# Expert weights converted through four staging pairs, an early list from 24 token tiles, and a second weight set asked for on its own

## The chip, the core and the metric

The kernel runs on one core of a Trainium2 chip. The metric is the device time of one execution in microseconds (us), taken as the median of several runs. A profiled execution, from which all rows come, is a run of its own and takes a little longer.

## What is computed

The reference chains three parts in float32:

```python
# 1 attention between x (8, 8, 512, 64) and 32 state rows per head, both ways
xread = softmax(scale * x @ state.T) @ state
sread = softmax(scale * state @ x.T) @ x
x = concat([xread, sread], rows)       # 8 * 544 = 4352 tokens of 512
# 2 a feed-forward layer: w_in (512, 2048), w_out (2048, 512)
g = relu(x @ w_in) ** 2
x = g @ w_out
# 3 one of 8 experts per token: w1 (8, 512, 1024), w2 (8, 1024, 512)
idx = argmax(cosine(x, expert_emb) / tau); gate = softmax(...)[idx]
out[token] = gate * (relu(x[token] @ w1[idx]) @ w2[idx])
```

The kernel keeps float32 accuracy by splitting each operand into two float16 halves, high and low, and adding three matmuls (high by high, high by low, low by high).

## The kernel before

The tokens lie in 34 tiles of 128: 32 of the x rows (NXT) and two of the state rows. Three stages overlap.

The attention goes through eight batches (`attention`, `state_side`). The first mixture (`up1`, `down1`) goes through 17 units of two token tiles: the up product of a unit in eight chunks c, the squared hidden chunk split into `g_h` and `g_l` by `hidden` (L1130 and L1136 on ScalarE, L1139 and L1141 on VectorE), and the down product of each tile in four pieces of 12 matmuls (L1219 to L1221). The last unit holds the state rows; its up product is L1174 to L1176. `route_tile` scales a finished tile into a record (`rec`), turns it with a DMA transpose into `xr` (L1017, one buffer, queue of SyncE) and forms the expert logits on TensorE (L1026 to L1028). `route_group` takes four tiles at once: some 30 small VectorE operations choose the expert and the place, advance the running counts `cum`, and GpSimd scatters the four records into device memory (L1105).

The second mixture (`moe2`) takes 128 tokens of one expert per step. `list_of` makes three lists of steps from the counts: list 0 with the first EARLY = 6 full tiles, taken from the first SEEN token tiles alone, list 1 with the other full tiles, list 2 with the rests in halves of 64. `gather` fetches the records of a step (L1456), `turn` transposes them (L1476), `up2` and `down2` multiply (L1527 to L1529, L1552), `finish` scales and scatters the result (L1504). Even steps use weight places of side 0 (`stage` for w1, `he` for w2), odd steps those of side 1 (`xx` and `sw`). `fetch_weights` loads them with SyncE: it reads the expert's number from the list and issues a 2 MB load that is skipped if the expert is the one already there (L1436).

`experts` brings w1 and w2 into the split form that `fetch_weights` reads. It loads halves of 1 MB into staging places (`stage`, one part of `wo_t`, and after the attention `xx`), finds a scale per matrix (L936), and converts 64 pieces of 128 by 1024: ScalarE makes the high half (L308), VectorE the low half (L303), both into a pair of buffers in the first half of `he` (`phl`, two pairs), and SyncE writes both halves, 256 KB each, to device memory (L325). A pair is free again when its write has landed. The second half of `he` belongs to the attention (`eb_v`) until that is over.

The order on every engine is fixed at build time by a planner (`Plan`). Each part of the kernel is a thread that yields (engine, duration); the planner always takes the thread that can start first, at a tie the one with the lower priority number. Events (`ev`) and slots order the threads, and `plan.dma(bytes)` books a transfer at 350 GB/s and 2 us to land. "attention" is the event after the last batch, "experts" that after the last conversion, "spare" that the part of `wo_t` in which the lists are computed is free, "moe1" that after the last down product. The priority number of the conversions is PRIO_E (4) during the attention and PRIO_E1 after it; routing has 2 and the lists 2.5.

Of the kernel before, what the change touches and what calls it, by code (L numbers as in the profile page):

```python
# [11 lines left out]
F16 = mybir.dt.float16  # L12
# [12 lines left out]
NT = NTOK // 128  # L25
NXT = B * S // 128
EARLY = 6
SEEN = 28
FULL = -(-(NTOK - NE * 127) // 128)
HT = 64  # L30
HALF = (NTOK - 128 * FULL + NE * (HT - 1)) // HT // 2 + 1
# [20 lines left out]
MARG = 1.75  # L52
GATE_E = ('xg', 1)
PRIO_E = 4
PRIO_E1 = 1.6
PRIO_SW = 1.4
TINY = 0.18

# [152 lines left out]
def act(n):  # L211
    return "act", 0.1 + 0.83e-3 * n
# [19 lines left out]
def moe_kernel(  # L232
# [19 lines left out]
    plan = Plan()  # L252
# [52 lines left out]
    def split(hi, lo, src, scale, n):  # L305

        yield act(n)
        nc.scalar.activation(out=hi, in_=src, func=AF.Copy, scale=scale)  # L308
        yield dve(n)
        split_lo(lo, src, scale, hi)  # L310
# [12 lines left out]
    def load(dst, src, nbytes):  # L323
        yield "sp", 0.06
        nc.sync.dma_start(dst, src)  # L325
        return plan.dma(nbytes)
# [35 lines left out]
    cum = const.tile([128, NT + 1, NE], F16, name="cum")  # L362
# [17 lines left out]
    def ev(*key):  # L380
        return evs.setdefault(key, Ev(plan))
# [7 lines left out]
    he = att.tile([128, 4096], I32, name="he")  # L389
# [4 lines left out]
    phl = he[:, 0:2048].bitcast(F16).rearrange("p (q a n) -> p q a n", q=2, a=2)  # L394
# [305 lines left out]
    stage_slots, phl_slots, pjk_slots = Slots(plan, 3), Slots(plan, 2), Slots(plan, 1)  # L700
# [167 lines left out]
    def tensor_scale(acc, s, inv):  # L868

        v = small.tile([128, 1], F32, name="fv")  # L870
        yield tiny(1)
        V.tensor_reduce(out=v, in_=acc, axis=X, op=ALU.add)
        at = plan.now()
        yield t_slots
        plan.cur[2] = max(at, plan.now())
        p = ps_t.tile([128, 512], F32, name="t")
        yield "pe", 0.1
        mm(p[:, 0:1], lhsT=one32, rhs=v, start=True, stop=True)
        w = small.tile([128, 1], F32, name="fw")
        yield tiny(4)  # L880
        V.tensor_scalar(out=w, in0=p[:, 0:1], scalar1=FLOOR, scalar2=None, op0=ALU.max)
        t_slots.release()
        pow2(s, inv, w, 204)


    def experts():


        yield ev(*GATE_E)
        halves = {}  # L890
        last = wo_t[:, NB:].rearrange("p q a k d -> p (q a k d)").bitcast(I32)
        places = [stages[0], stages[1], last]

        def put(t):
            if t is last and ev("attention").time is not None:
                ev("spare").set()
            else:
                places.append(t)
                stage_slots.release()

        def more():
            yield ev("attention")
            for i in range(2):
                put(xx[:, 2048 * i:2048 * i + 2048])

        def fetch():
            for n in range(4 * NE):
                yield stage_slots
                e, h = n // 4, n % 2
                t = places.pop(0)  # L910
                if t is last and ev("attention").time is not None:
                    put(t)
                    yield stage_slots
                    t = places.pop(0)
                halves[n] = t
                t = t.bitcast(F32)
                if n % 4 < 2:
                    v = w1[e].rearrange("(k p) f -> p k f", p=128)[:, 2 * h:2 * h + 2, :]
                else:
                    v = w2[e].rearrange("(k p) f -> p k f", p=128)[:, 4 * h:4 * h + 4, :]  # L920
                when = yield from load(t.rearrange("p (k f) -> p k f", k=v.shape[1]), v, 1 << 20)
                ev("stage", n).set(when)

        def scale():
            for i in range(2 * NE):
                acc = small.tile([128, 4], F32, name="pacc")
                if ev("attention").time is not None:
                    plan.cur[1] = PRIO_E1
                for n in range(2 * i, 2 * i + 2):
                    yield ev("stage", n)  # L930
                    for a in range(2):
                        yield pjk_slots
                        jk = att.tile([128, 1024], BF16, name="pjk")
                        col = 2 * (n % 2) + a
                        yield act(1024)
                        nc.scalar.activation(out=jk, in_=halves[n].bitcast(F32)[:, a * 1024:a * 1024 + 1024],  # L936
                                             func=AF.Square, accum_out=acc[:, col:col + 1])
                        pjk_slots.release()
                col = i // 2 + NE * (i % 2)
                yield from tensor_scale(acc, se[:, col:col + 1], ise[:, col:col + 1])  # L940
                ev("scale", i).set()

        plan.add(fetch(), PRIO_E)
        plan.add(more(), PRIO_E)
        plan.add(scale(), PRIO_E)
        for i in range(2 * NE):
            e, col = i // 2, i // 2 + NE * (i % 2)
            dst = (w1_d if i % 2 == 0 else w2_d)[e * 128:e * 128 + 128, :]
            yield ev("scale", i)
            if ev("attention").time is not None:  # L950
                plan.cur[1] = PRIO_E1
            for q in range(4):
                n = 2 * i + q // 2
                src = halves[n].bitcast(F32)[:, q % 2 * 1024:q % 2 * 1024 + 1024]
                at = plan.now()
                yield phl_slots
                plan.cur[2] = max(at, plan.now())
                hl = phl[:, q % 2]
                yield from split(hl[:, 0, :], hl[:, 1, :], src, se[:, col:col + 1], 1024)
                if q % 2 == 1:  # L960
                    put(halves.pop(n))
                at = plan.now()
                yield from load(dst[:, q * 1024:q * 1024 + 1024], hl[:, 0, :], 1 << 18)
                t = yield from load(dst[:, 4096 + q * 1024:4096 + q * 1024 + 1024], hl[:, 1, :], 1 << 18)
                phl_slots.release(t)
                plan.cur[2] = at
        ev("experts").set()

# [437 lines left out]
    def sides_of(t):  # L1406
        which, j = order[t]
        return (2, 3) if which == 2 else ((j + (EARLY if which else 0)) % 2,)

    def fetch_weights(t0, t1):  # L1410
        def fetch(name, done, ts, slots, src):
            last = None
            for t in ts:
                which, j = at_step(t)
                yield ev("tab", which)
                tab = lists[which]["tab"]
                if last is not None:
                    yield ev(done, last)
                elif which == 2:
                    last = HALF_AT - 6 if name == "w1" else HALF_AT - 5  # L1420
                    yield ev("moe1")
                    yield ev(done, last)
                else:
                    yield ev("experts")
                    yield ev("attention")
                    if name == "w2":
                        yield ev("up", 2 * B - 1)
                sides = sides_of(t)
                for i, a in enumerate(sides):
                    if i and last + 1 < t:  # L1430

                        yield ev(done, last + 1)
                    yield "sp", 0.15
                    ex = nc.sync.value_load(tab[0:1, i, j:j + 1], min_val=0, max_val=NE - 1)
                    new = nc.sync.value_load(tab[0:1, 2 + i, j:j + 1], min_val=0, max_val=1)
                    nc.sync.dma_start(slots[a], src[bass.ds(ex * 128, 128)], cond=new)  # L1436
                    when = plan.dma(2 << 20 if j == 0 and which != 1 else 1 << 19 if which == 2 else 1 << 18)
                last = t
                ev(name, t).set(when)

        for a in range(3):
            ts = [t for t in range(t0, t1) if sides_of(t)[0] == a]
            plan.add(fetch("w1", "up2", ts, w1s, w1v), 3)
            plan.add(fetch("w2", "down2", ts, w2s, w2v), 3)
# [3 lines left out]
    def gather(t0, t1, m2):  # L1448
        for t in range(t0, t1):
            which, j = at_step(t)  # L1450
            yield ev("idx", which)
            yield ev("records", (NT if which else SEEN) - 1)
            yield rec2_slots
# [6 lines left out]

            need = puts[:SEEN] if which == 0 else puts
            for put in need:
# [118 lines left out]
    def switch():  # L1581

        yield ev("cum", SEEN - 1)
        yield ev("spare")
        fetch_weights(0, NMAIN)
        yield from list_of(0, EARLY, SEEN)
        yield ev("up", 2 * B)
# [87 lines left out]
```

## Time and profile before

| | us |
|---|---|
| median of 3 runs (1145.3 to 1145.65) | 1145.32 |
| profiled execution | 1157.43 |
| its span, first to last instruction | 1155.6 |
| TensorE busy | 1032.8 (89%) |
| VectorE busy | 708.0 (61%) |
| ScalarE busy | 583.3 (50%) |

PE is TensorE's matmuls, PEld its weight loads, DVE VectorE, ACT ScalarE, POOL GpSimd, SP SyncE, SPq a queue entry of SyncE. Matmuls overlap, so the duration of one is longer than the step from one start to the next, and a busy share says less than the steps. The granted clock is a share of full speed (2.4 GHz); 0.50 is the lower level, 1.2 GHz. In brackets behind an instruction stands how long its engine was idle before it and whose end it waited for.

### The profile page before, as it was taken

Reading aid. Unit: us, or ns where it says so; the run is one execution under the profiler, and the core shown is the slowest. Engines: PE = TensorE matmul, PEld = TensorE weight load, DVE = VectorE, ACT = ScalarE, POOL = GpSimd, SP = SyncE. Lnnn points to the kernel's source line nnn. Section 1 sums busy time; section 2 is a strip of 40 time slices with the busy share of each in tenths; the row PEclk is TensorE's granted clock in tenths of the full one; section 3 lists DMA queues with packets and bytes.
Section 4 is the critical chain, followed back from the end, with each engine's and each line's share of the span. In section 5 each row is a group of like instructions: output and inputs, shape, how many; then the busy total and the mean of one; then the engine's idle time right before and its main releaser. Section 6 shows DMA issues by size and latency. Waiting matters only on the chain. (4 is left out here: it accounts for less than half of the span.)

```text
span 1155.6 us, 26458 instructions
## 1 busy us (share of the span) xinstructions
PE 1032.8 (89%) x10707; PEld 665.2 (58%) x10707; DVE 708.0 (61%) x1838; ACT 583.3 (50%) x959; POOL 126.2 (11%) x149
## 2 busy tenths in 40 slices
PE   2255899999999999999999999699999999999995
PEld 1134356555555555565555666377776777767773
DVE  6998877968869878688696784356422222222221
ACT  6689777776776977677777873111111111101110
POOL 0200000200100201002001010212121211211201
PEclk8579799999999999999999999899999999999998
DMA  9345466566685685656736676634696777685690
GB/s 354 112 151 128 151 159 211 105 193 145 183 223 125 209 238 157 189 117 183 238 71 229 205 232 273 167 92 93 209 297 173 204 213 206 185 250 155 179 295 28
DMA packets 160546, 211.77 MB, mean 183 GB/s; under 512 B 112226, under 2 KB 113506, under 8 KB 155171
## 3 DMA queue, kind: packets, MB, share of 16 engines
q1 hardware_dynamic: 152098, 182.94, 55.5%
q0 software_dynamic: 8320, 27.08, 7.2%
q8 instruction: 86, 1.41, 0.5%
q14 instruction: 42, 0.34, 0.1%
HBM read 257.92 MB, written 51.68 MB: 268 GB/s over the span
## 5 line engine op out<-in xcount | busy, mean ns | idle before, releaser
L1219 PE MATMUL d<-wo_t,g_h 128*128 128x512 f16 x544 | 209.7, 386 | 3.6 <-DVE g_h L1139 1.4
L1221 PE MATMUL d<-wo_t,g_l 128*128 128x512 f16 x544 | 209.3, 385 | 1.8 <-DVE l L1063 1.8
L1220 PE MATMUL d<-wo_t,g_h 128*128 128x512 f16 x544 | 209.5, 385 | 1.2 <-DVE wo_t L303 1.2
L1486 ACT ACTIVATE r<-u 128x512 f32<-128x512 f32 x70 | 41.8, 597 | 324.5 <-PE u L1529 300.0
L1167 PE MATMUL u<-aT,sw 128*128 128x256 f16 x512 | 141.5, 276 | 25.3 <-ACT r L1130 22.5
L1169 PE MATMUL u<-aT,sw 128*128 128x256 f16 x512 | 141.4, 276 | 0.9 <-DVE sw L303 0.9
L1168 PE MATMUL u<-aT,sw 128*128 128x256 f16 x512 | 141.3, 276 | 0.0
L1130 ACT ACTIVATE r<-u,cg 128x512 f32<-128x512 f32 x136 | 93.0, 684 | 72.9 <-PE u L1176 35.4
L1489 DVE CAST hh<-r 128x512 f16<-128x512 f32 x70 | 30.4, 434 | 136.5 <-ACT r L1486 134.4
L1105 POOL DMA_INDIRECT rec_d<-rec,pi x34 | 37.8, 1112 | 576.6 <-DVE f L1009 175.7
L1141 DVE TENSOR_TENSOR g_l<-r,g_h 128x512 f16<-128x512 f32 x136 | 93.3, 687 | 6.5 <-ACT r L1136 5.1
L1500 DVE TENSOR_SCALAR o<-d,rec,wo_t 128x512 f32<-128x512 f32 x35 | 28.3, 810 | 108.9 <-PE d L1552 99.2
L1221 PEld LDWEIGHTS <-g_l 128*128 128x128 f16 x544 | 53.9, 99 | 70.2 <-issue 5.3
L1552 PEld LDWEIGHTS <-hh 128*128 128x128 f16 (+1 forms) x688 | 54.7, 102 | 56.9 <-issue 0.4
L1136 ACT ACTIVATE r<-r 128x512 f32<-128x512 f32 x136 | 85.6, 629 | 1.9
L1219 PEld LDWEIGHTS <-g_h 128*128 128x128 f16 x544 | 54.2, 100 | 55.9 <-issue 5.7
L1220 PEld LDWEIGHTS <-g_h 128*128 128x128 f16 x544 | 53.8, 99 | 53.5 <-issue 5.0
L1139 DVE CAST g_h<-r 128x512 f16<-128x512 f32 x120 | 50.9, 424 | 47.8 <-ACT r L1136 44.7
L1527 PE MATMUL u<-xes,stage 128*128 128x128 f16 x448 | 75.9, 219 | 0.0
L1529 PE MATMUL u<-xes,stage 128*128 128x128 f16 x448 | 75.9, 219 | 0.0
L1528 PE MATMUL u<-xes,stage 128*128 128x128 f16 x448 | 75.9, 219 | 0.0
L1168 PEld LDWEIGHTS <-sw 128*128 128x128 f16 x512 | 50.6, 99 | 37.6 <-issue 26.5
(334 smaller groups left out, 2682.3 us busy)
## 6 DMA issues: line engine op xcount, KB each, us to landing
w_d<-he SPq DMA_DIRECT2D x128, 256.0 KB
wo_t<-w_d SPq DMA_DIRECT2D x16, 2048.0 KB
stage<-w_d SPq DMA_DIRECT2D x14, 2048.0 KB
he<-w_d SPq DMA_DIRECT2D x14, 2048.0 KB
xx<-w_d SPq DMA_DIRECT2D x13, 2048.0 KB
sw<-w_d SPq DMA_DIRECT2D x13, 2048.0 KB
stage<-in_w_dram SPq DMA_DIRECT2D x20, 1024.0 KB
g_h<-w_d SPq DMA_DIRECT2D x8, 2048.0 KB
```

The source lines that it names most:

```text
L1130: nc.scalar.activation(out=r, in_=ps, func=AF.Relu, scale=cg[:, g:g + 1])
L1136: nc.scalar.activation(out=r, in_=r, func=AF.Square)
L1141: V.tensor_tensor(out=gl, in0=r, in1=gh, op=ALU.subtract)
L1167: mm(o, lhsT=hl[:, i, 0, fs], rhs=aT[:, i, :], start=i == 0, stop=False)
L1168: mm(o, lhsT=hl[:, i, 0, fs], rhs=aT[:, 2 + i, :], start=False, stop=False)
L1169: mm(o, lhsT=hl[:, i, 1, fs], rhs=aT[:, i, :], start=False, stop=i == 1)
L1219: mm(ps, lhsT=g_h[:, f, ts], rhs=w[:, 0, :], start=f == 0, stop=False)
L1220: mm(ps, lhsT=g_h[:, f, ts], rhs=w[:, 1, :], start=False, stop=False)
L1221: mm(ps, lhsT=g_l[:, f, ts], rhs=w[:, 0, :], start=False, stop=f == KF - 1)
L1527: mm(p[:, j, xs], lhsT=w[:, 0, k, fs], rhs=xe[:, k, xs], start=k == 0, stop=False)
L1528: mm(p[:, j, xs], lhsT=w[:, 0, k, fs], rhs=xe[:, 4 + k, xs], start=False, stop=False)
L1529: mm(p[:, j, xs], lhsT=w[:, 1, k, fs], rhs=xe[:, k, xs], start=False, stop=k == 3)
```

## The change

`experts` views the whole of `he` as four half pairs instead of the first half as two. A deque `pairs` hands them out: 0 and 1 from the start, 2 and 3 are added with one slot each when the attention is over. PRIO_E1 goes from 1.6 to 2.2 and SEEN from 28 to 24. In `fetch_weights` the first load of w1 for step 1 waits, in the plan, for the counts of the last x tile ("cum" of NXT - 1), and that of w2 for "moe1"; before, both followed the same events as those of step 0. The planner books all four first loads of steps 0 and 1 with 2 MB, and the first loads of list 2 with 0.5 MB; before, 2 MB were booked for the first step of lists 0 and 2 and 0.25 MB for step 1.

```diff
-SEEN = 28
+SEEN = 24
-PRIO_E1 = 1.6
+PRIO_E1 = 2.2
@@ experts
+        halves_of = he.bitcast(F16).rearrange("p (q a n) -> p q a n", q=4, a=2)
+        pairs = deque((0, 1))
@@ more
             for i in range(2):
                 put(xx[:, 2048 * i:2048 * i + 2048])
+                pairs.append(2 + i)
+                phl_slots.release()
@@ the conversion of a piece
-                hl = phl[:, q % 2]
+                pair = pairs.popleft()
+                hl = halves_of[:, pair]
...
                 phl_slots.release(t)
+                pairs.append(pair)
@@ fetch_weights
                     if name == "w2":
                         yield ev("up", 2 * B - 1)
+                    if t == 1:
+
+                        yield ev("moe1") if name == "w2" else ev("cum", NXT - 1)
...
-                    when = plan.dma(2 << 20 if j == 0 and which != 1 else 1 << 19 if which == 2 else 1 << 18)
+                    when = plan.dma(2 << 20 if t < 2 else 1 << 19 if which == 2 else 1 << 18)
```

## Rows read from the trace of the kernel before

**Rows 1.** The page: span, and PE's busy tenths in 40 equal slices

```profile
span 1155.6 us, 26458 instructions
...
PE   2255899999999999999999999699999999999995
```

**Rows 2.** Table by slice: busy PE, PEld, DVE, ACT, POOL; clock; DMA share; GB/s

```profile
606.70:635.60 28.90, 26.32 (x213) 14.95 (x211) 19.13 (x42) 20.93 (x35) 3.02 (x7) 0.94 0.68 229
635.60:664.50 28.90, 28.69 (x208) 18.54 (x207) 21.42 (x60) 25.64 (x44) 0.00 (x0) 1.00 0.67 205
664.50:693.40 28.90, 28.69 (x199) 18.05 (x197) 24.72 (x89) 20.64 (x32) 4.61 (x7) 1.00 0.74 232
...
722.20:751.10 28.90, 18.79 (x116) 10.00 (x115) 10.14 (x51) 5.12 (x10) 6.28 (x7) 0.82 0.66 168
```

**Rows 3.** Timeline of PE around 725 us: start, duration, engine, line, operation

```profile
725.50 0.27 PE L1176 MATMUL u<-x_h,wi_l 128*128 128x256 f16 x1
732.63 0.19 PE L1026 MATMUL t<-en_h,xr 128*128 128x8 f16 x1 [6.85 <-DMA xr<-rec]
...
732.97 0.59 PE L1219 MATMUL d<-wo_t,g_h 128*128 128x512 f16 x1
...
736.63 0.38 PE L1219 MATMUL d<-wo_t,g_h 128*128 128x512 f16 x1
```

**Rows 4.** Timeline of SyncE's queue, 690 to 735 us

```profile
691.69 12.73 SPq L325 DMA_DIRECT2D w_d<-he  x8
706.47 0.37 SPq L1436 DMA_DIRECT2D stage<-w_d  x1
...
712.72 21.65 SPq L1017 DMA_TRANSPOSE xr<-rec  x2
```

**Rows 5.** Table by 2 us, columns as in Rows 2

```profile
720.00:722.00 2.00, 2.00 (x17) 1.51 (x16) 0.00 (x0) 0.09 (x1) 0.00 (x0) 1.00 1.02 426
...
726.00:728.00 2.00, 0.00 (x0) 0.00 (x0) 0.00 (x0) 0.00 (x0) 0.00 (x0) 1.00 0.98 384
...
734.00:736.00 2.00, 2.00 (x6) 0.70 (x5) 0.00 (x0) 0.00 (x0) 0.00 (x0) 0.50 0.68 131
```

**Rows 6.** Timelines of ACT, DVE and PE, 741 to 750 us

```profile
742.13 0.63 ACT L1136 ACTIVATE r<-r 128x512 f32<-128x512 f32 x1
...
741.69 0.17 DVE L1031 COPY lg<-t 128x8 f32<-128x8 f32 x1 [0.37 <-PE t L1028]
...
743.91 0.42 DVE L1139 CAST g_h<-r 128x512 f16<-128x512 f32 x1
...
746.09 0.68 DVE L1141 TENSOR_TENSOR g_l<-r,g_h 128x512 f16<-128x512 f32 x1
...
744.39 0.39 PE L1219 MATMUL d<-wo_t,g_h 128*128 128x512 f16 x1 [1.42 <-DVE g_h L1139]
...
746.83 0.61 PE L1221 MATMUL d<-wo_t,g_l 128*128 128x512 f16 x1 [1.84 <-DVE l L1063]
...
750.19 0.38 PE L1220 MATMUL d<-wo_t,g_h 128*128 128x512 f16 x1
```

**Rows 7.** The waits of the whole span: us in total, times, longest

```profile
PE u L1167 <- ACT r L1130: 22.5, 18, 2.8
```

**Rows 8.** Conversions after the attention: first on ACT, last on DVE

```profile
612.74 1.14 ACT L308 ACTIVATE he<-stage,se 128x1024 f16<-128x1024 f32 x1
...
702.77 1.28 DVE L303 SCALAR_TENSOR_TENSOR he<-xx,se,he 128x1024 f16<-128x1024 f32 x1
```

**Rows 9.** Timeline of PE: last down product, first uses of xx, third tile, sw

```profile
761.83 0.38 PE L1221 MATMUL d<-wo_t,g_l 128*128 128x512 f16 x1
...
765.40 0.22 PE L1527 MATMUL u<-xes,xx 128*128 128x128 f16 x1
...
776.29 0.22 PE L1527 MATMUL u<-xes,stage 128*128 128x128 f16 x1
...
781.68 0.38 PE L1552 MATMUL d<-sw,hh 128*128 128x512 f16 x1
```

## The prediction

> **What bounds the kernel now.** I began with the page. Its line of 40 slices shows TensorE (PE) at 9 nearly everywhere between the first five slices and the last; the one hole is the slice at 722 to 751 us [rows 1]. The table by slice gives its size: 18.79 us of PE work in 28.90 us at a mean granted clock of 0.82, where the slices before are full at 1.00 or nearly so [rows 2]. VectorE (DVE) and ScalarE are not full there, so this stretch is bound by PE, and a change to the weights can pay only through this hole. I went through the starts of all matmuls and counted as loss what a step from one start to the next takes beyond the usual 0.216 us (512 columns) or 0.11 us (256). From 612 to 722 us that finds four losses of 0.3 to 0.5 us, after 752 us ten of about 0.5, in the hole two large ones.
>
> Stall one runs from 725.50 to 732.63 us: PE wants the turned rows of token tile 30 (L1026) and waits for the transpose (xr<-rec) [rows 3]. On the queue of SyncE (SP) that transpose was issued at 712.72, right behind four weight loads of 2 MB, the first at 706.47 [rows 4]. The transfers run at 384 to 426 GB/s up to 728 us [rows 5]; 8.39 MB at some 410 GB/s are 20.5 us, most of the delay. PE loses 7.0 us (7.13 less 0.11), and afterwards it runs at clock 0.50, that is 1.2 of 2.4 GHz [rows 5]: nine matmuls from 732.97 to 736.63 take 3.66 us instead of 1.94 [rows 3]. Together 8.7 us.
>
> Stall two is DVE's doing. The logits of tile 31 come at 741.69, and the small routing operations of tiles 28 to 31 are put ahead of the split of the last hidden chunk (743.91 and 746.09), for which PE waits 1.42 and 1.84 us by the rows, 1.6 and 2.0 by the starts. Eight matmuls from 746.83 then take 3.36 us instead of 1.73 [rows 6]. Together 5.2 us. Without routing work 0.75 us would stay: ScalarE's square ends at 742.76, the cast (0.42) lets PE start at about 743.25 where it ran out at 742.81, and the subtract (0.68) holds it about 0.3 us more [rows 6].
>
> **The change part by part.** The plan that orders the instructions is the same until the attention is over, at about 612 us: the new half pairs and the priority act only from there on, and list 0 waits for "spare" besides. So the first 612 us cost and give nothing.
>
> *First weights of side 1 asked for apart.* Loads three and four (into xx and sw) leave their place ahead of tile 30's transpose. Ahead of it then stand 4.19 MB, 10.2 us at 410 GB/s: from 706.47 to about 717. The transpose landed some 4 us after the last load (728 to 732.6), so now near 721.5, and PE comes to L1026 at 725.61. Stall one is gone with 4 us to spare, even if nothing else moves: +8.7 us. The planner now books these two loads as 2 MB each, where it booked 0.25 MB each, 1.5 us for what takes 10.2. That is why it put L1026 too early. The loads' time on SP (four in 6.25 us [rows 4], so 1.6 each) leaves that place too.
>
> *Where they land.* w1 of step 1 now follows "cum" of tile 31, about 728 to 738 us, and takes 1.6 on SP, 5.1 of transfer and some 2 to land. PE first wanted xx at 765.40, so about 11 us earlier in the new run: 754.5. w2 follows "moe1", the last down matmul, at 761.83 before and 751 after, so it lands at 760; PE wanted sw at 781.68, now about 771 [rows 9]. Behind w2 on SP stand the transposes of tile 33 and of the third expert tile; the latter would land at about 761, and PE wants it at 776.29 less 11, 765.4 [rows 9]. I cost this at nothing; what hides it is the PE work of steps 0 and 1, with 4 us to spare at the tightest place. If that cover is gone it is rival C. The Trainium skill ("DMA: Bandwidth & Descriptors", section "Queues, rings and completion order") speaks against this part: a DMA engine consumes the descriptors of a ring in order, so a load asked for later still holds up all that is queued behind it. The trace agrees (the transpose of 712.72 waited out all four loads [rows 4]). By that rule alone the 10.2 us are moved and not removed, and the sum is rival C's; by the rows PE has other work at the new place, and the sum stands.
>
> *Four pairs instead of two, priority 2.2 instead of 1.6.* After the attention 19 pieces are converted from 612.74 to 704.05, one in 4.8 us [rows 8], and the last eight writes go out from 691.69 on [rows 4]. A piece costs 1.14 us of ScalarE and 1.28 us of DVE [rows 8] for any number of pairs; the new pairs take away the wait for a pair's write. DVE is idle for 9.8, 7.5 and 4.2 us of the slices from 606.70 on [rows 2]. Packed into half of that, the last piece is done about 10 us earlier, at 694 (bounds: 704, no gain, and 683, no idle time left). On PE this is worth nothing by itself, as the second mixture begins later. Its price is that denser conversions come in the way of the hidden chunks' work. Over the whole span PE waited for L1130 18 times, 22.5 us in all, 2.8 at most, and nearly always during the attention [rows 7]; after it, once, 0.2 us. I take -1.0 us, nearer to the stretch after the attention; bounds 0 and -4, a mean wait of 1.25 us in each of three slices. The routing of tiles 24 to 27, which gave way to the conversions at 1.6, now goes ahead of them; nobody waits for its records before the first gather at 741.65, so that is worth nothing.
>
> *Early list from 24 tiles.* "cum" of tile 23 is there before the attention ends, so the list starts with "spare", at about 623 us, and is in time for a first load at 694 or later, as it was for that at 706.47. It is the same work, and by the reference's inputs all six early tiles are of expert 0 for 24 tiles as for 28: lists and switches of weights are unchanged. The gathers wait for the pool that opens after the last up product, as before. Zero. The third list's first loads, booked as 0.5 MB instead of 2, don't reorder PE, for which the second mixture is one thread: zero, bounds +-0.5 us.
>
> *Stall two.* Tile 31's transpose waits for tile 30's L1026 (one buffer), so its logits came 9 us after 732.63. With stall one gone they come while PE is one or two chunks further back, and the small operations (21 at 0.2 us) meet a chunk behind which PE has a down product of 2.6 us in hand. Bounds: all 5.2 us stay, or 0.75. I take 2.0 us left, nearer to the floor, since the meeting came of the late transpose: +3.2 us.
>
> **Sum.** 8.7 + 3.2 - 1.0 = 10.9 us. The profiled execution took 1157.43 us (the span of 1155.6 and 1.8 around it), and would take 1146.5. The median of the runs, 1145.32, is 12.1 us lower; PE's steps are the same in both, so I take off the same microseconds: 1134.4, forecast 1134.5.
>
> **Rivals.**
> A: stall two stays whole, as the planner again lets the routing start just before the last chunk: 8.7 - 1.0 = 7.7, so 1137.6. For it: such operations run as soon as they are ready, in the order of the plan. Against: the same coincidence is needed.
> B: the conversions crowd out the hidden chunks: the longest wait seen (2.8 us [rows 7]) in each of three slices, 8.4 us, and stall two unchanged: 8.7 - 8.4, so about 1145, no change. Against: after the attention PE mostly has the other unit's down product to turn to.
> C, the slower end: the two moved loads stand ahead of transposes for which PE has already come. Each is 5.1 us of queue, both 10.2, and two spells at 1.2 GHz cost 3.3 more (1.7 and 1.6 above), against 8.7 saved: -4.8, so 1150. It decides once PE's work after the last down product runs short by more than the 4 us above.
> D: the pairs don't speed the conversions, because DVE or the transfers set their pace. Stall one still goes (the 4 us at tile 30), nothing crowds, but the routing shifts less and 4 us of stall two stay: 8.7 + 1.2 = 9.9, so 1135.5.
>
> **How the numbers follow.** Forecast 0.50, A 0.18, D 0.12, B 0.10, C 0.10. The range leaves out C and most of B: from both stalls down to the floor (8.7 + 4.45, and the small losses after 612 us, 1131) up to A with the crowding at its bound (8.7 - 4 = 4.7, 1140.6) and a part of B: 1131 to 1142. A measurement of this kernel tells 0.2% (2.3 us) from no change. Faster by more: forecast, A, D and a little of B, 0.82; within: most of B, 0.08; slower: C, 0.10.
>
> **What would show it.** Right: no wait of L1026 for xr<-rec above 1 us between 700 and 770; on SP two weight loads, then transposes, then the loads of xx and sw singly; a full clock at 722 to 751; the last conversion near 694. Wrong: first up products that wait for xx, sw or xes; waits for L1130 that add up between 612 and 700; PE at clock 0.50 in a new place.

## The result, and the profile after

The changed kernel takes 1133.99 us (median of 4 runs, 1130.1 to 1137.14) where the kernel before takes 1145.49 beside it (4 runs, 1145.3 to 1152.02): a ratio of 0.9876 with a 95% interval of 0.9841 to 0.9911. Measured again in 5 rounds beside the first experiments, the ratio is 0.9861 (0.9831 to 0.9891). The profiled execution took 1136.58 us. Behind the edits in `experts`, line numbers of the changed kernel stand 6 to 9 higher (L1026 is L1032, L1130 is L1136, L1219 to L1221 are L1225 to L1227, L1436 is L1445, L1527 is L1536).

The page of the changed kernel, and its table by slice with the columns of [rows 2]:

```profile
span 1134.7 us, 26451 instructions
...
PE   2245799999999999999999999999999999999995
...
606.70:635.60 28.90, 27.28 (x220) 15.82 (x216) 22.11 (x72) 18.94 (x30) 2.80 (x5) 1.00 0.72 216
...
722.20:751.10 28.90, 28.90 (x288) 19.97 (x286) 14.63 (x63) 7.52 (x15) 10.55 (x11) 1.00 0.84 200
```

The hole of [rows 1] is closed: PE is full from 722 to 751 us at clock 1.00, where it had 18.79 us of work at 0.82 [rows 2]. SyncE's queue shows the new order, tile 30's transpose ahead of the first loads, tile 31's between the second and the third:

```profile
696.76 1.26 SPq L1023 DMA_TRANSPOSE xr<-rec  x1
698.44 0.85 SPq L325 DMA_DIRECT2D w_d<-he  x2
701.46 0.37 SPq L1445 DMA_DIRECT2D stage<-w_d  x1
703.54 0.35 SPq L1445 DMA_DIRECT2D he<-w_d  x1
712.44 1.26 SPq L1023 DMA_TRANSPOSE xr<-rec  x1
715.75 0.35 SPq L1445 DMA_DIRECT2D xx<-w_d  x1
...
741.00 0.36 SPq L1445 DMA_DIRECT2D sw<-w_d  x1
```

On the timeline of PE, from 612 us to the early steps of the second mixture (784 us), there is one wait of more than a microsecond, for ScalarE, and one small one for a transpose. Tiles 30 and 31 (704.55 and 719.17) pass without a wait:

```profile
621.06 0.27 PE L1173 MATMUL u<-aT,sw 128*128 128x256 f16 x1 [1.62 <-ACT r L1136]
...
704.55 0.17 PE L1032 MATMUL t<-en_h,xr 128*128 128x8 f16 x1
...
719.17 0.17 PE L1032 MATMUL t<-en_h,xr 128*128 128x8 f16 x1
...
752.67 0.18 PE L1032 MATMUL t<-en_h,xr 128*128 128x8 f16 x1 [0.54 <-DMA xr<-rec]
```

Stall two is gone too. On VectorE (DVE) the logits of tile 31 come 8 us before the split of the last hidden chunk (L1145), and the routing of tiles 28 to 31 has advanced its counts (L1082) before that split:

```profile
719.79 0.16 DVE L1037 COPY lg<-t 128x8 f32<-128x8 f32 x1
...
726.42 0.76 DVE L1082 TENSOR_TENSOR cum<-cum,oh 128x8 f16<-128x8 f16 x4
...
727.69 0.42 DVE L1145 CAST g_h<-r 128x512 f16<-128x512 f32 x1
```

To compare kernels I count PE's loss as the prediction did: what a step from one matmul's start to the next takes beyond the usual one for its columns, from 26 us after the start of tile 24's squares to the ninth r of the second mixture. It was 15.8 us and is now 3.9. The two profiled executions lie 20.9 us apart (1157.43 and 1136.58), more than the medians. Some 12 us of that are this loss; 2.3 us are there before the two programs differ in order (tile 24's squares start at 588.57 and 586.32 us), and the rest lies around 605 to 612 us and in short pauses of the second mixture, which come and go between executions.

### The profile page after: what moved, and what is told of

Same layout as the page of the kernel before. It is cut to its first block, busy times and chain, and to the rows that moved or that the text cites. A ratio compares the mean times of both kernels' runs of the same rounds, so it can differ in the third digit from the quotient of the medians.

```text
span 1134.7 us, 26451 instructions
## 1 busy us (share of the span) xinstructions
PE 1025.5 (90%) x10707; PEld 663.7 (58%) x10707; DVE 706.3 (62%) x1838; ACT 583.1 (51%) x959; POOL 128.1 (11%) x149
## 5 line engine op out<-in xcount | busy, mean ns | idle before, releaser
L1225 PE MATMUL d<-wo_t,g_h 128*128 128x512 f16 x544 | 207.6, 382 | 1.7 <-ACT wo_t L862 0.8
L1226 PE MATMUL d<-wo_t,g_h 128*128 128x512 f16 x544 | 207.4, 381 | 1.2 <-DVE wo_t L303 1.2
L1227 PE MATMUL d<-wo_t,g_l 128*128 128x512 f16 x544 | 207.2, 381 | 0.0
L1136 ACT ACTIVATE r<-u,cg 128x512 f32<-128x512 f32 x136 | 92.6, 681 | 53.4 <-PE u L1175 33.5
L1227 PEld LDWEIGHTS <-g_l 128*128 128x128 f16 x544 | 53.5, 98 | 66.6 <-issue 3.1
L1225 PEld LDWEIGHTS <-g_h 128*128 128x128 f16 x544 | 53.9, 99 | 53.0 <-issue 3.2
L1145 DVE CAST g_h<-r 128x512 f16<-128x512 f32 x120 | 50.7, 423 | 41.2 <-ACT r L1142 41.0
L1536 PE MATMUL u<-xes,stage 128*128 128x128 f16 x448 | 75.9, 219 | 0.0
```

Source lines behind the costliest of these rows:

```text
L1136: nc.scalar.activation(out=r, in_=ps, func=AF.Relu, scale=cg[:, g:g + 1])
L1225: mm(ps, lhsT=g_h[:, f, ts], rhs=w[:, 0, :], start=f == 0, stop=False)
L1226: mm(ps, lhsT=g_h[:, f, ts], rhs=w[:, 1, :], start=False, stop=False)
L1227: mm(ps, lhsT=g_l[:, f, ts], rhs=w[:, 0, :], start=False, stop=f == KF - 1)
L1536: mm(p[:, j, xs], lhsT=w[:, 0, k, fs], rhs=xe[:, k, xs], start=k == 0, stop=False)
```

## The experiments

All ratios are to the kernel before on the same chip in 5 rounds. Its median there was 1159.88 us in the first group, 1155.54 in the second and 1145.76 in the third. The losses are each of one profiled execution.

### First group: the loads, and what is left without them

**The two edits of the loads alone**, on the kernel before:

```
+                    if t == 1:
+                        yield ev("moe1") if name == "w2" else ev("cum", NXT - 1)
...
-                    when = plan.dma(2 << 20 if j == 0 and which != 1 else ...
+                    when = plan.dma(2 << 20 if t < 2 else ...
```

> The kernel before with the two edits of fetch_weights alone: side 1's first loads wait in the plan, and the planner books 2 MB for each first load. Pairs, priority and early list as before. Theory Q (the two loads queued ahead of tile 30's transpose make the hole, and stall two follows from the late transpose): stall one goes, 8.7 us, and 0 to 4.5 us of stall two, so 1132 to 1137. Theory R (what counts is that the expert weights are ready sooner, so pairs, priority and list make the gain): under 1 us of gain, 1144 or more.

Measured: 0.9981 (0.9956 to 1.0005), loss 13.35 us. The ratio is theory R's, no clear gain, but not for its reason: tile 30 no longer waits, stall two stays, and tile 32 waits instead. PE, then SyncE's queue:

```profile
730.40 0.39 PE L1219 MATMUL d<-wo_t,g_h 128*128 128x512 f16 x1 [0.95 <-DVE g_h L1139]
732.86 0.61 PE L1221 MATMUL d<-wo_t,g_l 128*128 128x512 f16 x1 [1.86 <-DVE g_l L1141]
...
752.52 0.19 PE L1026 MATMUL t<-en_h,xr 128*128 128x8 f16 x1 [3.32 <-DMA xr<-rec]
```

```profile
735.73 0.33 SPq L1439 DMA_DIRECT2D xx<-w_d  x1
736.44 3.55 SPq L1479 DMA_TRANSPOSE xes<-rec  x1
741.05 4.81 SPq L1017 DMA_TRANSPOSE xr<-rec  x1
```

The load of xx went out at 735.73 us and stands ahead of tile 32's transpose: the mechanism of rival C, at a place where I had not looked for a reader. GpSimd's four scatters of records run at the same time (742.54 to 747.45 us); their share in this wait was not measured apart. The clock falls with it (by 2 us, columns as in [rows 2]):

```profile
750.00:752.00 2.00, 0.00 (x0) 0.00 (x0) 0.00 (x0) 0.00 (x0) 0.00 (x0) 1.00 0.99 208
752.00:754.00 2.00, 1.48 (x24) 1.48 (x25) 0.60 (x5) 0.00 (x0) 0.00 (x0) 0.60 1.12 293
754.00:756.00 2.00, 2.00 (x23) 2.00 (x22) 0.99 (x2) 1.17 (x2) 0.00 (x0) 0.55 0.94 401
```

**The changed kernel without these two edits** (pairs, priority and early list stay; the diff is the one above, reversed).

> The changed kernel without the two edits of fetch_weights: four pairs, priority 2.2 and the list from 24 tiles stay, the four first loads stand in one row again. Theory Q: the row is issued some 5 us earlier, as the conversions end earlier (first load at 701.5 in the changed kernel against 706.5), so stall one shrinks from 8.7 to some 2 to 5 us and stall two may stay: 1137 to 1142. Theory R: the whole gain is here, 1133 to 1136.

Measured: 0.9941 (0.9916 to 0.9967), loss 12.35 us. The four loads stand in a row from 699.73 to 705.55 and tile 31's transpose behind them, so the long wait is back, one tile later; stall two is gone. The ratio is in theory Q's range, with the parts the other way round: Q had stall one shrink and let stall two stay:

```profile
725.92 0.19 PE L1032 MATMUL t<-en_h,xr 128*128 128x8 f16 x1 [7.04 <-DMA xr<-rec]
```

**The booking alone.** The plan counts 2 MB for the loads of step 1, and nothing waits that did not wait before:

```
-                    when = plan.dma(2 << 20 if j == 0 and which != 1 else ...
+                    when = plan.dma(2 << 20 if t == 1 or j == 0 and which != 1 else ...
```

> The kernel before with the booking alone: the planner books 2 MB instead of 0.25 MB for the first two loads of side 1, which stay ahead of tile 30's transpose. The transposes still come 10 us later than with two loads, but the planner now knows and puts L1026 later. Theory Q, with the planner's ignorance as the cause of the wait: L1026 no longer stops PE, but the routing of tiles 28 to 31 moves towards the last down products, so part of the loss comes back there: 1137 to 1142. Rival (booking is all that matters): the same as e1 within 1 us. Rival (booking changes nothing as the data are late anyway): 1144 to 1147.

Measured: 0.9899 (0.9865 to 0.9933), loss 8.65 us; the strongest of the single edits measured, and better than all three ranges. The loads still go out in a row and tile 30's transpose still follows them, and yet PE does not wait for it (SyncE's queue, then PE):

```profile
707.32 0.37 SPq L1436 DMA_DIRECT2D stage<-w_d  x1
709.41 0.35 SPq L1436 DMA_DIRECT2D he<-w_d  x1
711.27 0.34 SPq L1436 DMA_DIRECT2D xx<-w_d  x1
713.12 0.34 SPq L1436 DMA_DIRECT2D sw<-w_d  x1
713.56 11.26 SPq L1017 DMA_TRANSPOSE xr<-rec  x1
```

```profile
698.73 0.17 PE L1026 MATMUL t<-en_h,xr 128*128 128x8 f16 x1
736.65 0.17 PE L1026 MATMUL t<-en_h,xr 128*128 128x8 f16 x1
747.79 0.18 PE L1026 MATMUL t<-en_h,xr 128*128 128x8 f16 x1 [2.23 <-DMA xr<-rec]
```

Between the routing of tile 29 and that of tile 30 PE now does 37.9 us of other work (698.73 to 736.65). In the kernel before these lay at 697.88 and 732.63, of which 7.0 were the wait, so some 27.7 us of work. The plan, told of the 2 MB, put 10 us more of the hidden chunks ahead of tile 30. Tile 31 then waits 2.2 us, and there is a wait of 2.3 us for ScalarE at 682.08, ahead of the weight loads.

**The changed kernel again**, beside these.

> The changed kernel once more, for the spread of its runs (1130.1 to 1137.1 so far) and for the comparison with e1 and e2 on one chip: 1131 to 1137 in both theories.

Measured: 0.9861 (0.9831 to 0.9891), loss 3.45 us. Against the version without the load edits on the same chip that is 1144.55 to 1152.75, 8.2 us.

### Second group: list, pairs, priority

**The list from 24 tiles alone** (`SEEN = 24`), on the kernel before.

> The kernel before with the list from 24 tiles alone. Theory S: as e2, that is the wait of L1026 for xr<-rec stays at some 7 us behind four loads in a row, now for tile 31 in place of 30, and the wait for the last hidden chunk goes: ratio 0.992 to 0.997. Theory P: no change, 0.998 to 1.002.

Measured: 1.0000 (0.9976 to 1.0023), loss 19.1 us. The wait for a transpose stays (6.75 us, now for tile 31, as theory S said), stall two stays in part (0.39 and 1.33 us), and the first expert tile is waited for 2.00 us. The ratio is theory P's.

**List from 24 tiles and the load edits**, with two pairs and priority 1.6.

> The kernel before with the list from 24 tiles and the two edits of fetch_weights; two pairs and priority 1.6 as before. Theory S (the early list is the second half of the gain: its VectorE work leaves the stretch before the first loads, so tile 30's transpose stands ahead of them, and the routing of tiles 28 to 31 comes clear of the last hidden chunk): a ratio to the kernel before of 0.985 to 0.990, that of the whole change (0.9861). Theory P (pairs and priority do that, by ending the conversions sooner): as e1, 0.995 to 1.0.

Measured: 0.9921 (0.9890 to 0.9951), loss 7.84 us, between the two theories. No transpose is waited for, stall two partly stays:

```profile
735.42 0.39 PE L1219 MATMUL d<-wo_t,g_h 128*128 128x512 f16 x1 [0.76 <-DVE g_h L1139]
737.41 0.39 PE L1221 MATMUL d<-wo_t,g_l 128*128 128x512 f16 x1 [1.38 <-DVE g_l L1141]
```

**The changed kernel with the list from 28 tiles** (`SEEN = 28`).

> The changed kernel with the list from 28 tiles again; pairs, priority and the edits of fetch_weights stay. Theory S: the list's work comes back before the first loads, they are issued later and the routing meets the last chunk again: ratio 0.991 to 0.998. Theory P: 0.984 to 0.988, as the whole change. (In the plan's order tile 30's transpose stays just ahead of the loads here, which speaks for P.)

Measured: 0.9963 (0.9939 to 0.9988), loss 12.6 us. The first expert tile now comes late:

```profile
746.15 0.27 PE L1536 MATMUL u<-xes,stage 128*128 128x128 f16 x1 [4.39 <-DMA xes<-rec]
```

The ratio is theory S's, its reason is not: the first load isn't issued later (113.4 us after tile 24's squares, 115.1 in the changed kernel), and of stall two only 0.61 us come back. Nor are the gathers late. In both kernels, as in every version here, the first gather starts 0.28 us after the last up product ends. What differs is how soon PE comes for the tile: here 3.7 us after the last up product, in the changed kernel 15.4, as the plan puts fewer down products between. The last up matmul, GpSimd's first gather and (for the changed kernel) PE's first use; first with the list from 28 tiles, then the changed kernel:

```profile
737.82 0.27 PE L1182 MATMUL u<-x_h,wi_l 128*128 128x256 f16 x1
738.37 1.07 POOL L1465 DMA_INDIRECT rec<-rec_d,wo_t  x1 [49.91 <-DVE rec L1107]
```

```profile
725.91 0.27 PE L1182 MATMUL u<-x_h,wi_l 128*128 128x256 f16 x1
726.46 1.07 POOL L1465 DMA_INDIRECT rec<-rec_d,wo_t  x1 [48.44 <-PE u L1182]
741.61 0.22 PE L1536 MATMUL u<-xes,stage 128*128 128x128 f16 x1
```

**The changed kernel with the old priority** (`PRIO_E1 = 1.6`).

> The changed kernel with the conversions at priority 1.6 again, ahead of the routing. In the plan's order tile 30's transpose is back behind the first two loads. Theory S: as the list is early, it costs little: 0.985 to 0.991. Theory P, priority as its part: 0.993 to 0.999. Both: on the chip only 10 us of load stand ahead of tile 30 and PE has 4 us to spare, so L1026 doesn't wait.

Measured: 0.9874 (0.9838 to 0.9910), loss 5.96 us, as theory S said, and L1026 doesn't wait: the new priority adds nothing that can be measured. This version differs from the one with list and load edits by the four pairs alone: 0.9874 against 0.9921 on the same chip (1141.11 and 1146.81 us, 5.7 us). The first load goes out at 694.95 us instead of 712.18 (13 us earlier, counted from tile 24's squares), and stall two is gone.

### Third group: place or plan

**The load edits, with both loads of step 1 behind "moe1" in the plan**, on the kernel before:

```
+                    if t == 1:
+                        yield ev("moe1") if name == "w2" else ev("moe1")
```

> Kernel before with the change's two edits of fetch_weights, but with both second-step loads (xx and sw) held until the last hidden chunk is planned, so that the transposed copies of tiles 30 to 33 all go ahead of xx in SyncE's queue. The earlier run with xx between tiles 31 and 32 lost 13.35 us between tile 24 and the second mixture's step 5, 3.3 us of it in the wait for tile 32's copy and about as much in the halved clock behind it. Theory V (the place of the loads in the queue decides): both waits for a token tile's copy are gone, stall two (about 5 us) stays, the loss is 7 to 10 us and the ratio 0.993 to 0.996. Rival W (the plan's order brings another wait whichever load is moved): a new wait of 2 us or more appears in 720 to 760 and the ratio stays at 0.997 to 0.999.

Measured: 0.9907 (0.9872 to 0.9943), loss 11.1 us. No token tile waits for its transpose any more. Stall two stays, and step 1 waits for its weights:

```profile
727.93 0.39 PE L1221 MATMUL d<-wo_t,g_l 128*128 128x512 f16 x1 [1.87 <-DVE g_l L1141]
747.51 0.29 PE L1530 MATMUL u<-xes,xx 128*128 128x128 f16 x1 [2.48 <-DMA xx<-w_d]
```

The ratio is a little better than theory V said, the loss a little larger: both theories had a part, since a new wait did appear, and taking tile 32's wait away paid all the same (0.9907 against 0.9981, on two chips).

**The same in the changed kernel.**

> Changed kernel with xx held in the same way (both second-step loads behind the last hidden chunk). Theory V: nothing waits for xx before about 750 us, so the time is the changed kernel's, ratio 0.985 to 0.989, with no wait over 1 us between 690 and 780. Rival W: the load then stands ahead of the first expert tiles' copies, a wait of 2 us or more for xes appears, and the ratio is 0.990 to 0.994.

Measured: 0.9901 (0.9870 to 0.9932), loss 6.77 us, with a new wait of 2.91 us for the first expert tile's transpose. It is the wait that rival W named, but not for its reason: that transpose, the first of the two below, stands ahead of xx in SyncE's queue. PE came for the tile 5.2 us after the last up product, and the plan set that:

```profile
726.64 3.21 SPq L1485 DMA_TRANSPOSE xes<-rec  x2
...
734.86 0.35 SPq L1445 DMA_DIRECT2D xx<-w_d  x1
```

The ratio stands at the edge of W's range, near V's, and doesn't tell the theories apart.

**The changed kernel without the added waits, with the booking.**

> Changed kernel without the wait added to fetch_weights, with the booking kept: the four 2 MB loads stand in a row again, tile 30's copy ahead of them and tile 31's behind. Theory V (the place in the queue decides): the wait of about 7 us of the version without both edits returns and the ratio is 0.993 to 0.996. Theory B (what decides is that the plan counts 2 MB for each load, and so routes tile 31 later): no wait over 2 us for a token tile's copy, ratio 0.986 to 0.990.

Measured: 0.9893 (0.9855 to 0.9931), loss 6.12 us: theory B. The loads stand in a row, tile 31's transpose behind them, and PE finds it landed (SyncE's queue, then PE):

```profile
703.66 0.34 SPq L1442 DMA_DIRECT2D sw<-w_d  x1
708.89 6.49 SPq L1023 DMA_TRANSPOSE xr<-rec  x1
```

```profile
701.01 0.17 PE L1032 MATMUL t<-en_h,xr 128*128 128x8 f16 x1
724.77 0.17 PE L1032 MATMUL t<-en_h,xr 128*128 128x8 f16 x1
```

The version without booking and without waits issues the same transpose at the same place, behind the load of 705.55, and PE comes to it after 16.1 us of work (702.78 to 718.9), 7 us too early. Here it comes after 23.8.

**The four pairs alone**, on the kernel before (list from 28 tiles, priority 1.6, loads unchanged).

> Kernel before with the four pairs of halves alone (list from 28 tiles, priority 1.6, loads unchanged). Prediction's theory (pairs are worth nothing by themselves, since the conversions are off the path): stalls one and two stay as before and the ratio is 0.998 to 1.002. Rival P (earlier conversions move the plan's work in the last tiles): stall two shrinks to under 2 us and the ratio is 0.993 to 0.997.

Measured: 0.9986 (0.9964 to 1.0008), loss 17.6 us, as the prediction's theory said: both stalls stay. The last conversion starts 99.1 us after tile 24's squares instead of 114.2, 15 us earlier, but the first load goes out at 699.96, 17 us after that conversion. In between SyncE waits for the list (waits on SyncE, 684 to 702 us: us in total, times, longest):

```profile
SPq L1440 <- DVE wo_t L1376: 12.0, 1, 12.0
```

### All versions together

| version | list | pairs | prio | booked | waits | ratio | loss, us |
|---|---|---|---|---|---|---|---|
| before | 28 | 2 | 1.6 | no | no | 1 | 15.8 |
| list alone | 24 | 2 | 1.6 | no | no | 1.0000 | 19.1 |
| pairs alone | 28 | 4 | 1.6 | no | no | 0.9986 | 17.6 |
| load edits alone | 28 | 2 | 1.6 | yes | yes | 0.9981 | 13.4 |
| changed, list from 28 | 28 | 4 | 2.2 | yes | yes | 0.9963 | 12.6 |
| changed, without load edits | 24 | 4 | 2.2 | no | no | 0.9941 | 12.4 |
| list and load edits | 24 | 2 | 1.6 | yes | yes | 0.9921 | 7.8 |
| load edits, both loads later | 28 | 2 | 1.6 | yes | later | 0.9907 | 11.1 |
| changed, both loads later | 24 | 4 | 2.2 | yes | later | 0.9901 | 6.8 |
| booking alone | 28 | 2 | 1.6 | step 1 | no | 0.9899 | 8.7 |
| changed, no added waits | 24 | 4 | 2.2 | yes | no | 0.9893 | 6.1 |
| changed, old priority | 24 | 4 | 1.6 | yes | yes | 0.9874 | 6.0 |
| changed | 24 | 4 | 2.2 | yes | yes | 0.9861 | 3.5 |

The order by ratio is nearly the order by loss, and from one end to the other the loss falls by 12 us and the time by 11.5 (first measurement) or 15.3 (beside the first group): the change works through this stretch of PE, as [rows 2] said that it must. The lowest seven ratios have intervals that overlap. No version measured beats the changed kernel. The added waits without the booking, and the priority alone, were not measured.

## Why the prediction was right, and where it was not

**The bound and the size.** Both stalls were the loss, and both are gone. The medians fell by 11.5 us where the sum said 10.9. That the forecast of 1134.5 meets 1133.99 to half a microsecond is luck: two misses cancel. The profiled execution fell by 20.9 us and not by 10.9, and the one of after lies 2.6 us above its median and not 12.1. A profiled execution isn't always the longer one: that of the load edits alone (1150.02) lies below its median (1156.68). Nor do the terms add up as the sum has them: load edits, pairs and list each give nothing clear by themselves.

**Stall one, 8.7 us.** The size held: putting the load edits back into the rest of the change brings 8.2 us. Two things in the step were wrong. "Stall one is gone with 4 us to spare, even if nothing else moves" holds for tile 30 only; with nothing else moved the ratio is 0.9981, not clear of no change, because the load of xx met tile 32's transpose. I had called that rival C and costed it at nothing, with the cover read from the tightest later place (the third expert tile) and not from tile 32, which stood nearer. The Trainium skill ("DMA: Bandwidth & Descriptors", section "Queues, rings and completion order") states that a DMA engine consumes the descriptors of a ring in order. The version with the load edits alone agrees: issuing tile 32's transpose took 4.81 us behind xx, where one alone takes 1.24 to 1.26. The second error is the reason. I named the booking ("that is why it put L1026 too early") and then credited the loads' new place. The booking alone gives 0.9899, and without the added waits the change still has 0.9893. By these values the plan's knowledge of the bytes does most of it, by laying PE's work over the transfer. What the waits add on top (0.9893 in the third group, 0.9861 and 0.9876 before) is within the intervals and stays open.

**Where the moved loads land.** In the changed kernel nothing waited for xx or sw, as costed; a load of xx held longer made step 1 wait 2.48 us in one version.

**Pairs, "worth nothing by itself".** Alone they do give nothing (0.9986), and they do bring the conversions forward, by 15 us in place of the 10 taken. In company they were undervalued: on top of list and load edits they bring 5.7 us; stall two goes and the loads come earlier, but the losses of the two profiled executions account for 1.9 us of it, and the rest stays open. In the changed kernel the last conversion is only 2.9 us earlier than before (111.3 us after tile 24's squares in place of 114.2), and with priority 1.6 7.9 us earlier (106.3). The pairs win 13 to 15 us (15 alone; from 119.3 to 106.3 beside list and load edits), the early list gives back 4 to 6 of it (107.7 to 111.3 in the changed kernel, 112.9 to 119.3 beside the load edits) and the priority 5, at no measurable cost. So rival D's premise was half true in the kernel as changed, for another reason than D named. The crowding, -1.0 us, isn't shown. The losses between 612 us and tile 30's squares rose from 1.9 to 3.4 us, above all by the wait of 1.62 us at 621.06. But that wait is not in the second profiled execution of the same kernel, and it stands, 34.7 us after tile 24's squares as here, in a version that has neither pairs nor priority (the load edits with both loads later, PE in the order of the kernel before up to 714 us there):

```profile
615.27 0.27 PE L1167 MATMUL u<-aT,sw 128*128 128x256 f16 x1 [1.62 <-ACT r L1130]
```

So it differs between executions and can't be put down to the change.

**Early list, "zero".** True alone (1.0000), false in the sum: I argued that the list from 28 tiles was in time for a load at 706, and did not ask whether it would be for an earlier one. With the pairs alone it was not: SyncE waited 12.0 us for it, and the first load went out 116.5 us after tile 24's squares where it was 117.9. In the changed kernel a list from 28 tiles costs 0.9963 against 0.9874 for the version beside it, which has priority 1.6. There SyncE doesn't wait for the list; the plan puts PE's step 0 closer behind the last up product, and PE waits 4.39 us for the first expert tile. This is the term that I missed most: it was read against the kernel before and not against the moved work.

**Stall two, 2.0 us left.** None is left. The direction held, the reason only partly. I tied it to tile 30's late transpose; but it stays in versions where no transpose is late (list and load edits, 0.76 and 1.38 us; both loads moved, 0.95 and 1.87) and goes in one where a transpose waits 7.04 us. Between two versions that differ by the pairs alone it goes with the pairs. The traces show what sets it. In the six versions with stall two (before; load edits alone; list alone; pairs alone; list and load edits; load edits with both loads later) the logits of tile 31 come 1.6 to 4.5 us before ScalarE's last square ends, so the routing falls on the last split. In five others they come 7.1 to 12.4 us before it, in the changed kernel 8.4, and the routing has advanced its counts before that split; with the booking alone and without the added waits the plan puts the routing behind the split. So the condition that I named (the logits come while PE is a chunk or two further back) was right. What brings it is the plan's place for tile 31, not the end of the late transpose.

**Rivals.** A (stall two stays) and C (the moved loads stand in the way) both came true in the load edits alone, at 0.9981, and neither in the whole change. B did not come.

## What to carry to other kernels

Where a planner orders the work, an under-booked transfer is a stall of its own: correct the cost it counts before you move the transfer, and look for how much other work it then lays over it (here 10 us for 4 MB). Cost an edit against the schedule that the other edits leave and not only against the one in the trace: the list was in time for the old loads and held up the ones that four pairs alone would have let go 12 us earlier. When one wait is taken from an in-order queue, look for the next reader behind each load at its new place, beginning with the nearest.

## What the runs showed of the hardware that I had not expected

- The same order of instructions does not give the same times. Up to the attention's end all versions issue in the same order, and yet tile 24's squares started between 580.5 us (both loads moved) and 594.3 us (list from 28 tiles in the changed kernel). The kernel before had medians of 1145.5 to 1159.9 us on the chips used. Only ratios within a group say something below 1%.
- The clock did not fall by the length of the wait alone. After 2.91 us (the changed kernel with later loads) the windows around it show 1.00; after 2.48 us (the same on the kernel before) the next one shows 0.51; after 2.00 us (the list alone) 0.92 and then 0.50; after 3.32 us 0.60 and 0.55. So part of a stall's price, half speed for some microseconds behind it, comes with some waits of 2 to 3 us and not with others. The two windows right behind the first two of these waits, columns as in [rows 2]:

```profile
731.00:733.00 2.00, 2.00 (x28) 1.64 (x29) 0.16 (x1) 0.00 (x0) 1.40 (x2) 1.00 1.15 316
...
747.00:749.00 2.00, 1.49 (x15) 1.49 (x16) 0.00 (x0) 0.00 (x0) 0.00 (x0) 0.51 1.02 426
```
